# The output projection as side by side 64-row products, in a gated attention unit followed by a token mixer

## The chip, the core and the metric

The kernel runs on one core of a Trainium2 chip. The metric is device time in microseconds (us), from the first to the last instruction of the program on that core. Before the change three runs took 780.02, 781.06 and 780.99 us, median 780.99.

The core has five engines with a queue of instructions each. PE multiplies matrices: it loads weights and streams rows past them, and its sums appear in PSUM. ACT and DVE work element by element, and alone of the engines beside PE read PSUM here. POOL works element by element on SBUF. SP issues most of the transfers. Each engine takes its instructions in the order in which the program gives them, and waits at an instruction until all that it needs is there.

## What is computed

Inputs are u, v (8 x 3200 x 256), z (8 x 3200 x 64) and three small weights. Cut to what matters, for each of the 8 batches:

```
scores = (1 / S) * z @ z.T                 # S = 3200: 3200 x 3200
attn   = max(scores, 0) ** 2
x      = u * (attn @ v)                    # 3200 x 256
wq, wk = x @ w_q, x @ w_k                  # 3200 x 64 each
W_tok  = (1 / 8) * wq @ wk.T
mixed  = W_tok @ x                         # done as wq @ (wk.T @ x)
out    = max(mixed, 0) @ w_out             # 256 x 256 weight: the output projection
```

The change is in the last line: the output projection contracts over the 256 columns of max(mixed, 0).

## The kernel before, in words

Each batch is cut into seven groups of rows: six of 512 and one of 128. For the attention, score tiles are made in pairs (`use_pair`, `scores`, L265): two products of 64 contracted rows, one in the upper half and one in the lower half of the PE array. ACT or DVE takes the pair out of PSUM with a relu (L287, L291), ACT or POOL squares it into one of 16 tiles `at` (L307, L309), and these tiles, or their transposes `tt`, are the weights of the second product with v (L352, `acc`). The second product too runs as two 64-row halves beside each other, r = 0 and r = 1, each into its own bank of PSUM. When a group of rows is summed, ACT and DVE add the two halves (L368, L369), POOL multiplies by u (L388), SP transposes, and PE makes queries and keys (L417) and the heads wk.T @ x (L454), whose sum over the groups is known when the batch ends.

Then, while the attention of the next batch goes on, the batch before is finished group by group. `use_mix` makes mixed.T for a group (L482), ACT takes it out with a relu as `rt` (L503). `use_projs` multiplies `rt` by `wo` (L513): products over all 128 rows of the array, 8 of them for a 512-row group and 2 for the 128-row group, into a buffer `fo` of two banks. ACT or DVE takes `fo` out (L540, L535), and SP stores it. The groups come in twos (`PAIRED`): two 512-row groups are projected in one go, 16 matmuls, each with a buffer of its own.

PSUM has eight banks. Four hold `acc`. The other four are two buffers of two banks, shared by all else: score pairs (`sc`), queries and keys with heads (`qk`), `mx`, `fo`. They come from the pool `pps`, with `bufs=2` and one name, so they are taken in turn, and one is free again when its reader (ACT or DVE) is done.

The order of all instructions is written out beforehand by a planner in the kernel (L575 to L1037). It keeps a clock for each engine, `slots` for the two PSUM buffers, lists of `extras` (keys, heads, mix, proj) with the time from which they may run, and `moves` for SP with due times. At each step the loop at L1001 takes an extra, or a score pair where the supply of `at` tiles is behind (`wanted`), or one step of the second product (`acc_step`, two matmuls). An extra or a pair is taken only when a buffer is free in the planner's count (`room`) and ACT or DVE are free in time for the end of the running sum (`calm_for`). After the loop the last batch is finished in a tail of its own, with `proj` and `mixed` on what is then free.

Of the kernel before, what the change touches and what calls it, by code (L numbers as in the profile page):

```python
# [16 lines left out]
def kernel(  # L17
# [56 lines left out]
    pacc = ctx.enter_context(tc.tile_pool(name="pacc", bufs=1, space=bass.MemoryType.PSUM))  # L74

    def ps_tile(name):
# [47 lines left out]
    def turn_first(c):  # L124
        n0, nn = ZCH[c]
        if c < 3:
            tp = acc_tile((c + 1) // 2 % 2, c % 2, "ztp", FP16)
        else:
            open_slot()
            tp = pps.tile([P, 4 * W], FP16, tag="ps", name="ztp")  # L130
        for i in range(nn):
            nc.tensor.transpose(
                tp[:, ts(i, P)], zd0[:, n0 + i, :, :].rearrange("p a k -> p (a k)"), ident
            )
        clock[PE] += 0.055 * cold() * nn
        ready = clock[PE] + FROM_PE
        on_act = max(clock[ACT], ready) < max(clock[DVE], ready)
        copy = nc.scalar.copy if on_act else nc.vector.tensor_copy
        copy(out=zT[0][:, ds(n0 * P, nn * P)], in_=tp[:, 0 : nn * P])
        z_at[c] = give(ACT if on_act else DVE, ready, 0.16 + 0.07 * nn)  # L140
        if c == 3:
            close_slot(z_at[c])

    def warm(n):
        for _ in range(n):
# [359 lines left out]
    def proj(b, gi, banks):  # L505
        rt = rts.pop((b, gi))
        nj = widths[gi] // P
        for r in halves(gi):
            n = min(2, nj - 2 * r)
            flat = rt[:, r, :, :].rearrange("p d s -> p (d s)")  # L510
            for dc in range(ND):
                for j in range(n):
# [5 lines left out]
                        stop=(dc == ND - 1 and j == n - 1),  # L518
                    )

    def proj_out(b, gi, banks, ways, stores=None, at=0):
        n0 = starts[gi] // P
        if stores is None:
            fo = pg.tile([P, 2, W], FP32, tag="g", name="fo")
        else:
            fo = pg.tile([P, 2, W], FP32, tag="fo", name="fo", bufs=2)
        flat_out = fo[:].rearrange("p a w -> p (a w)")
        for on_dve, queue, n in ways:
            sl = slice(at * D, (at + n) * D)
            if isinstance(banks, list):  # L530
                part = banks[at // 2][:, 0 : n * D]
            else:
                part = banks[:].rearrange("p a w -> p (a w)")[:, sl]
            if on_dve:
                nc.vector.tensor_scalar(  # L535
                    out=flat_out[:, sl], in0=part, scalar1=FINAL_SCALE, scalar2=None,
                    op0=AOP.mult,
                )
            else:
                nc.scalar.mul(out=flat_out[:, sl], in_=part, mul=FINAL_SCALE)  # L540
# [39 lines left out]
        clock[engine] = max(clock[engine], ready) + weight  # L580
        return clock[engine] + HOP

    slots = [0.0, 0.0]
# [4 lines left out]
    mixed_at = []  # L588
    MIXES = 18.0
    MIXES_END = 14.0  # L590
    PAIRED = [0, 1, 2, 3, 4, 5]
    last = B - 1

    moves = []
# [21 lines left out]
    def add_extra(t, kind, fn):  # L616
        extras.append((t, kind, fn))
        extras.sort(key=lambda x: x[0])
# [18 lines left out]
    def close_slot(t):  # L637
        slots.append(t)

    def cold():  # L640
        return 2.0 if clock[PE] < 8.4 else 1.0
# [11 lines left out]
        return a + BIAS < d  # L653

    def use_pair():
        open_slot()
# [12 lines left out]
        g = first_stage(p, sc, ways)  # L669
        close_slot(done)  # L670
        pending.append((done, p, g))

    def squares():
# [34 lines left out]
        double_keys(b, gi)  # L708

    def use_keys(b, gi):  # L710
        open_slot()
        ps = ps_tile("qk")
        prior = None
        if keyed and keys_at.get(keyed[0], 1e9) <= clock[PE]:
# [23 lines left out]
        close_slot(done)  # L738
        if len(keyed) == 2 and gi == LASTG:
            add_extra(done + 14.0, "heads", use_heads)  # L740
        if final:
# [1 line left out]
                add_extra(done, "heads", use_heads)  # L743

    def use_heads():
        open_slot()
# [9 lines left out]
        close_slot(done)  # L756

    def heads_known(b):
        t = clock[PE]
# [2 lines left out]
                add_extra(t + 4.0 + (MIXES if b < last - 1 else MIXES_END) * i, "mix", lambda gi=gi: use_mix(b, gi))  # L762

    def use_mix(b, gi):
        open_slot()
# [5 lines left out]
        close_slot(done)  # L771
# [7 lines left out]
    def use_projs():  # L779
        some = mixed_at[:]  # L780
        mixed_at.clear()
        banks = []
        clock[PE] += 0.22
        for _, b, gi in some:
            open_slot()
            ps = ps_tile("fo")
            proj(b, gi, [ps[:, 0, :], ps[:, 1, :]])
            clock[PE] += 0.86 if gi < LASTG else 0.22
            banks.append((b, gi, ps, clock[PE] + FROM_PE))
        for i, (b, gi, ps, ready) in enumerate(banks):  # L790
            project_out(b, gi, ps, ready)

    def project_out(b, gi, ps, ready):
        stores = []
        on_act = max(clock[ACT], ready) + BIAS <= max(clock[DVE], ready) + 0.2
        proj_out(b, gi, ps, [(not on_act, nc.sync, widths[gi] // P)], stores)
        engine, t = (ACT, 1.0) if on_act else (DVE, 1.23)
        done = give(engine, ready, t if gi < LASTG else 0.3)
        close_slot(done)
        stored.append(1e9)  # L800

        def landed(t, i=len(stored) - 1):
            stored[i] = t

        move(done + SLACK, done + 6.0, 0.55, 1.6, stores[0], landed)

    def push(takes):
        give(POOL, clock[PE], 0.6)
# [139 lines left out]
    def calm_for(kind):  # L948
# [5 lines left out]
        if kind == "keys":  # L954
            return max(clock[ACT], ready + 0.66) + 0.56 <= t
        if kind == "proj":
            n = len(mixed_at)
            return max(clock[ACT], ready + 0.86 * n) + 1.03 <= t
        return max(clock[ACT], ready) + 1.03 <= t

    def p_chunk(p):
# [39 lines left out]
    while groups or work or current["left"]:  # L1001
        flush()
        squares()
        now = clock[PE]
        room = slots[0] <= now
# [12 lines left out]
        if extra and extra[1] == "proj":  # L1018
            room = slots[len(mixed_at) - 1] <= now
        p = produced[0]  # L1020
        able = p < NPAIR and z_here(p) and z_at[p_chunk(p)] <= now and (p < NAT or all_used(p - NAT) and turned_at.get(p - NAT, 0.0) <= now and not out_of.get(p - NAT))
        wanted = able and p * total < (done_acc + lead) * NPAIR
        if room and extra and calm_for(extra[1]) and (not wanted or turn_about or extra[1] == "proj"):
            turn_about = False
            extras.remove(extra)
            extra[2]()
# [5 lines left out]
        elif room and able and calm_for("pair"):  # L1032
            use_pair()
        else:
            marks = slots + [sp_at[0] - 0.4] + [x[0] for x in pending + later + extras + moves]
            marks += list(free_at.values()) + [t for t in row_at.values() if t > now][:50]
            clock[PE] = min([t for t in marks if t > now] + [now + 0.5])  # L1037

    while extras or later or moves:
        x = next((x for x in extras if x[1] == "proj"), None)
        if not x:
            ripe = [
                x
# [13 lines left out]
        else:  # L1059
            extras.remove(x)  # L1060
            x[2]()
    assert not pending and len(keyed) == 1
    def mixed(b, gi, i=None):
        if i is None:
            ps = ps_tile("mx")
# [22 lines left out]
    use_heads()  # L1088
# [57 lines left out]
```

## Time and profile before

| what | value |
|---|---|
| runs | 780.02, 781.06, 780.99 us; median 780.99 |
| profiled execution | 780.02 us; its span from first to last instruction is 780.0 us |
| PE busy | 765.9 us, 98% of the span |
| ACT, DVE, POOL busy | 558.1, 490.5, 619.5 us |
| granted PE clock | 0.998 of full speed over the span |

The profiled execution is the fastest of the three, 0.97 us under the median. In the profile, PE is a row of matmuls and PEld a row of weight loads that run beside them. A matmul of 64 rows is marked 64*128, one over the whole array 128*128. The matmuls are pipelined: a row of one lasts 269 to 273 ns, but the next begins long before it ends, so what a group costs PE is read from the starts of rows that follow each other, not from the sum of their lengths. "Issue" is a wait for which the profile shows no releaser.

### The profile page before, as it was taken

Reading aid. Unit: us, or ns where it says so; the run is one execution under the profiler, and the core shown is the slowest. Engines: PE = TensorE matmul, PEld = TensorE weight load, DVE = VectorE, ACT = ScalarE, POOL = GpSimd, SP = SyncE. Lnnn points to the kernel's source line nnn. Section 1 sums busy time; section 2 is a strip of 40 time slices with the busy share of each in tenths; the row PEclk is TensorE's granted clock in tenths of the full one; section 3 lists DMA queues with packets and bytes.
Section 4 is the critical chain, followed back from the end, with each engine's and each line's share of the span. In section 5 each row is a group of like instructions: output and inputs, shape, how many; then the busy total and the mean of one; then the engine's idle time right before and its main releaser. Section 6 shows DMA issues by size and latency. Waiting matters only on the chain.

```text
span 780.0 us, 28286 instructions
## 1 busy us (share of the span) xinstructions
PE 765.9 (98%) x12410; PEld 674.0 (86%) x12410; DVE 490.5 (63%) x506; ACT 558.1 (72%) x672; POOL 619.5 (79%) x518
## 2 busy tenths in 40 slices
PE   8999999999999999999999999999999999999996
PEld 6889989988888888988889888898888988999894
DVE  6576768767565766655657556575566765656534
ACT  6786785676877776876678777787778578777644
POOL 7798887668986978887779769887888868887850
PEclk9999999999999999999999999999999999999999
DMA  7899999999999999999899999999989999989725
GB/s 181 157 152 175 162 160 170 171 187 180 222 183 190 200 218 204 151 170 217 198 171 193 168 221 168 199 161 171 241 159 208 162 196 211 157 169 168 183 81 198
DMA packets 307116, 141.11 MB, mean 181 GB/s; under 512 B 285744, under 2 KB 288432, under 8 KB 306992
## 3 DMA queue, kind: packets, MB, share of 16 engines
q1 hardware_dynamic: 300224, 123.13, 85.8%
q0 software_dynamic: 6624, 15.98, 14.6%
q8 instruction: 97, 1.59, 0.9%
q14 instruction: 27, 0.22, 0.1%
q10 hardware_dynamic: 144, 0.20, 0.1%
HBM read 59.64 MB, written 26.21 MB: 110 GB/s over the span
## 4 chain that ended last, share of the span: by engine, by line
PE 94%; DVE 2%; DMA 1%; ACT 1%; issue 1%; POOL 0%; DVEq 0%; SPq 0%
PE acc L352 68%; PE sc L265 13%; PE fo L513 6%; PE qk L417 3%; PE qk L454 2%; PE mx L482 1%; DVE g L291 1%; DMA v_sb<-in_v_dram 1%; ACT g L287 1%; DVE both L369 0%; DVE fo L535 0%; DMA z<-in_z_dram 0%; ACT at L307 0%; PE xtx L555 0%; PE hd L454 0%
## 5 line engine op out<-in xcount | busy, mean ns | idle before, releaser
L352 PE MATMUL acc<-v_sb,at 64*128 64x256 f16 x7344 | 506.0, 269 | 2.3 <-issue 1.5
L309 POOL TENSOR_TENSOR at<-g 128x1024 f16<-128x1024 f32 (+2 forms) x240 | 432.5, 1813 | 88.0 <-DVE g L291 46.8
L352 PEld LDWEIGHTS <-at 64*128 64x128 f16 x7344 | 403.9, 94 | 54.5 <-issue 9.7
L291 DVE TENSOR_SCALAR g<-sc 128x1024 f32<-128x1024 f32 (+2 forms) x302 | 349.9, 1175 | 121.8 <-PE sc L265 109.8
L307 ACT ACTIVATE at<-g 128x1024 f16<-128x1024 f32 (+2 forms) x242 | 241.6, 1015 | 25.0 <-DVE g L291 22.5
L287 ACT ACTIVATE g<-sc 128x1024 f32<-128x1024 f32 (+2 forms) x177 | 174.8, 990 | 56.2 <-PE sc L265 50.9
L265 PE MATMUL sc<-zT 64*128 64x512 f16 x924 | 185.3, 375 | 2.4 <-DVE g L291 1.2
L388 POOL TENSOR_TENSOR x_sb<-both,u_sb 128x512 f16<-128x512 f32 (+1 forms) x112 | 134.3, 1205 | 48.9 <-DVE both L369 48.4
L352 PE MATMUL acc<-v_sb,tt 64*128 64x256 f16 x2272 | 168.0, 269 | 0.0
L352 PEld LDWEIGHTS <-tt 64*128 64x128 f16 x2272 | 127.0, 94 | 10.3 <-issue 0.6
L369 DVE TENSOR_TENSOR both<-acc,both 128x512 f32<-128x512 f32 (+1 forms) x104 | 69.5, 670 | 70.9 <-ACT both L368 62.0
L368 ACT COPY both<-acc 128x512 f32<-128x512 f32 (+1 forms) x104 | 58.9, 566 | 66.5 <-PE acc L352 63.1
L265 PEld LDWEIGHTS <-zT 64*128 64x128 f16 x924 | 62.2, 94 | 9.8 <-issue 5.2
L535 DVE TENSOR_SCALAR fo<-fo 128x1024 f32<-128x1024 f32 (+2 forms) x31 | 32.7, 1067 | 41.4 <-PE fo L513 41.3
L503 ACT ACTIVATE rt<-mx 128x1024 f16<-128x1024 f32 (+1 forms) x49 | 45.5, 931 | 12.2 <-PE mx L482 12.0
L430 ACT CAST qk<-qk 128x512 f16<-128x512 f32 (+1 forms) x54 | 29.4, 544 | 29.2 <-PE qk L454 25.4
L513 PE MATMUL fo<-wo,rt 128*128 128x256 f16 x400 | 49.4, 273 | 0.1
L469 DVE TENSOR_TENSOR ha<-qk,ha 128x512 f32<-128x512 f32 x37 | 25.6, 691 | 36.1 <-ACT qk L430 35.8
L513 PEld LDWEIGHTS <-rt 128*128 128x128 f16 x400 | 36.4, 98 | 10.8 <-issue 6.5
L540 ACT ACTIVATE fo<-fo 128x1024 f32<-128x1024 f32 (+2 forms) x27 | 24.6, 914 | 19.8 <-PE fo L513 19.8
L417 PE MATMUL qk<-xT_sb,wqk 64*128 64x256 f16 (+1 forms) x404 | 32.2, 265 | 0.0
L454 PE MATMUL qk<-x_sb,kx 64*128 64x256 f16 x360 | 29.1, 269 | 0.0
(44 smaller groups left out, 237.0 us busy)
## 6 DMA issues: line engine op xcount, KB each, us to landing
u_sb<-in_u_dram SPq DMA_DIRECT2D x48, 512.0 KB, 5.0
out_dram<-fo SPq DMA_DIRECT2D x46, 512.0 KB, 4.4
v_sb<-in_v_dram POOLq DMA_DIRECT2D x35, 320.0 KB, 6.2
zn<-in_z_dram POOLq DMA_DIRECT2D x7, 400.0 KB, 6.3
tt<-at SPq DMA_TRANSPOSE x143, 4.5
u_sb<-in_u_dram SPq DMA_DIRECT2D x8, 128.0 KB, 3.6
out_dram<-fo SPq DMA_DIRECT2D x8, 128.0 KB, 3.5
out_dram<-fo SPq DMA_DIRECT2D x4, 256.0 KB, 4.2
```

The lines of the kernel that those rows point to most:

```text
L265: nc.tensor.matmul(out=sc[:, h, 0:gw], lhsT=z_cols(b, h, ti * P, P), rhs=z_cols(b, h, gs, gw), start=True, stop=True,)
L287: nc.scalar.activation(out=g[:, hs, 0:w], in_=sc[:, hs, 0:w], func=RELU, scale=GSCALE)
L291: nc.vector.tensor_scalar(out=g[:, hs, 0:w], in0=sc[:, hs, 0:w], scalar1=0.0, scalar2=GSCALE, op0=AOP.max, op1=AOP.mult,)
L307: nc.scalar.square(out=out, in_=g[:, hs, 0:w])
L309: nc.gpsimd.tensor_mul(out=out, in0=g[:, hs, 0:w], in1=g[:, hs, 0:w])
L352: nc.tensor.matmul(out=accs[half, r][:, ds((j % 2) * D, D)], lhsT=weights(b, gi, ti, j)[top(r), :], rhs=vs[b][top(r), ti, :], start=(first ...
L368: nc.scalar.copy(out=both[:, 0 : n * D], in_=accs[half, 0][:, 0 : n * D])
L369: nc.vector.tensor_add(out=both[:, 0 : n * D], in0=accs[half, 1][:, 0 : n * D], in1=both[:, 0 : n * D])
L388: nc.gpsimd.tensor_mul(out=xs[b, gi][:, 0:n, :, r, :].rearrange("p n c d -> p (n c) d"), in0=both[:, 0 : n * D].rearrange("p (m d) -> p m ...
L417: nc.tensor.matmul(out=ps[:, r, 0 : n * P], lhsT=wqk[top(r), c, :, :].rearrange("p t h -> p (t h)"), rhs=xTs[b, gi][top(r), 0:n, c, :], st ...
L503: nc.scalar.activation(out=out, in_=ps[:, 0:nr, 0 : ND * n * P], func=RELU)
L513: nc.tensor.matmul(out=banks[r][:, ds(j * D, D)], lhsT=flat[:, ds((dc * n + j) * P, P)], rhs=wo[:, dc, :], start=(dc == 0 and j == 0), sto ...
```

## The change

Three things change together. The output projection of the first seven batches is cut into 64-row products. The projection of a 512-row group becomes two phases of 8 matmuls (`proj_phase`). In the first, rows 0 to 63 of the array work on bank 0 and rows 64 to 127 on bank 1. In the second, the halves change banks. Each bank so gets the sum over both halves. Between the phases stands a copy of two numbers out of the two banks (`mark`), on ACT or DVE, which the second phase waits for. The buffer stays taken from the first phase until the result is out. The 128-row group (`use_small_proj`) lets each half write its own bank and ACT and DVE add the two.

The groups are projected one by one instead of in twos: `PAIRED` and `mixed_at` go, the first phase is an extra `proj`, the second an extra `proj2`. `proj2` may run without a free buffer, since it has one, but in the planner it waits until the store before the last has landed (`stored[-2] + 2.0`). A mix may run while fewer than two groups are mixed and not yet projected out.

The two PSUM buffers get names, `ps0` and `ps1`, each a pool of one. `open_slot` takes the one that is free first by the planner's count.

```diff
-    pps = ctx.enter_context(tc.tile_pool(name="pps", bufs=2, space=bass.MemoryType.PSUM))
+    pps = ctx.enter_context(tc.tile_pool(name="pps", bufs=1, space=bass.MemoryType.PSUM))
...
     def ps_tile(name):
-        return pps.tile([P, 2, W], FP32, tag="ps", name=name)
+        if ending:
+            slot[0] = 1 - slot[0]
+        return pps.tile([P, 2, W], FP32, tag=f"ps{slot[0]}", name=name)
...
+    def proj_phase(b, gi, ps, crossed):
+        rt = rts.pop((b, gi)) if crossed else rts[b, gi]
+        for i, (dc, j) in enumerate((dc, j) for dc in range(ND) for j in range(2)):
+            for r in range(2):
+                bank = 1 - r if crossed else r
+                flat = rt[:, bank, :, :].rearrange("p d s -> p (d s)")
+                nc.tensor.matmul(
+                    out=ps[:, bank, ds(j * D, D)],
+                    lhsT=flat[top(r), ds((dc * 2 + j) * P, P)],
+                    rhs=wo[top(r), dc, :],
+                    start=(not crossed and i == 0),
+                    stop=(i == 3),
+                    skip_group_check=crossed,
+                )
+
+    def proj_parted(b, gi, ps):
+        flat = rts.pop((b, gi))[:, 0, :, :].rearrange("p d s -> p (d s)")
+        for dc in range(ND):
+            for r in range(2):
+                nc.tensor.matmul(
+                    out=ps[:, r, 0:D],
+                    lhsT=flat[top(r), ts(dc, P)],
+                    rhs=wo[top(r), dc, :],
+                    start=(dc == 0),
+                    stop=(dc == ND - 1),
+                )
...
     def open_slot():
-        clock[PE] = max(clock[PE], slots.pop(0))
+        slot[0] = k = min(slots, key=lambda k: slots[k])
+        clock[PE] = max(clock[PE], slots[k])
+        slots[k] = 1e9
+        return k
...
-        mixed_at.append((done, b, gi))
-        if gi in PAIRED:
-            if len(mixed_at) == 2:
-                add_extra(done + 0.5, "proj", use_projs)
-        else:
-            add_extra(done + 0.5, "proj", use_projs)
...
+        unprojected.append(gi)
+        use = use_proj if gi < LASTG else use_small_proj
+        add_extra(done + 0.5, "proj", lambda: use(b, gi))
+
+    def use_proj(b, gi):
+        k = open_slot()
+        ps = ps_tile("fo")
+        proj_phase(b, gi, ps, False)
+        clock[PE] += 0.44
+        mark = psml.tile([1, 2], FP32, tag="mark", name="mark")
+        ready = clock[PE] + FROM_PE
+        on_act = clock[ACT] < min(clock[DVE], shut())
+        copy = nc.scalar.copy if on_act else nc.vector.tensor_copy
+        copy(out=mark[:], in_=ps[0:1, :, D])
+        done = give(ACT if on_act else DVE, ready, 0.2)
+        add_extra(done + 0.2, "proj2", lambda: use_proj2(b, gi, k, ps))
+
+    def use_proj2(b, gi, k, ps):
+        proj_phase(b, gi, ps, True)
+        clock[PE] += 0.44
...
+        proj_out(b, gi, ps, [(not on_act, nc.sync, widths[gi] // P)], stores)
+        done = give(ACT, ready, 1.0) if on_act else give(DVE, ready, 1.23)
+        projected_out(k, done, stores[0])
+
+    def use_small_proj(b, gi):
+        k = open_slot()
+        ps = ps_tile("fo")
+        proj_parted(b, gi, ps)
...
+        nc.scalar.mul(out=fo[:, 1, 0:D], in_=ps[:, 1, 0:D], mul=FINAL_SCALE)
+        nc.vector.scalar_tensor_tensor(
+            out=fo[:, 0, 0:D], in0=ps[:, 0, 0:D], scalar=FINAL_SCALE,
+            in1=fo[:, 1, 0:D], op0=AOP.mult, op1=AOP.add,
+        )
...
-                and (x[1] != "proj" or all(t + 2.0 <= now for t in stored[-2:][: len(mixed_at)]))
+                and (x[1] != "proj2" or len(stored) < 2 or stored[-2] + 2.0 <= now)
                 and (x[1] != "heads" or keys_at.get(keyed[0], 1e9) <= now)
-                and (x[1] != "mix" or not any(y[1] == "proj" for y in extras))
+                and (x[1] != "mix" or len(unprojected) < 2)
...
-        if room and extra and calm_for(extra[1]) and (not wanted or turn_about or extra[1] == "proj"):
+        if (room or extra and extra[1] == "proj2") and extra and calm_for(extra[1]) and (not wanted or turn_about or extra[1] == "proj2"):
```

More of the change, by code (lines that the diff above doesn't have):

```diff
@@ L128, in turn_first @@
         else:
-            open_slot()
-            tp = pps.tile([P, 4 * W], FP16, tag="ps", name="ztp")
+            k = open_slot()
+            tp = pps.tile([P, 4 * W], FP16, tag=f"ps{k}", name="ztp")
         for i in range(nn):
@@ L793, in project_out @@
[L793 to L799, printed above, removed]
+        close_slot(k, done)
+        unprojected.append(gi)
+        use = use_proj if gi < LASTG else use_small_proj
+        add_extra(done + 0.5, "proj", lambda: use(b, gi))
@@ new lines, in use_proj2 @@
+    def use_proj2(b, gi, k, ps):
+        proj_phase(b, gi, ps, True)
+        clock[PE] += 0.44
+        ready = clock[PE] + FROM_PE
+        on_act = max(clock[ACT], ready) + BIAS <= max(clock[DVE], ready) + 0.2
+        stores = []
+        proj_out(b, gi, ps, [(not on_act, nc.sync, widths[gi] // P)], stores)
+        done = give(ACT, ready, 1.0) if on_act else give(DVE, ready, 1.23)
+        projected_out(k, done, stores[0])
+    def use_small_proj(b, gi):
+        k = open_slot()
+        ps = ps_tile("fo")
+        proj_parted(b, gi, ps)
+        clock[PE] += 0.22
+        fo = pg.tile([P, 2, W], FP32, tag="fo", name="fo", bufs=2)
+        nc.scalar.mul(out=fo[:, 1, 0:D], in_=ps[:, 1, 0:D], mul=FINAL_SCALE)
[3 more added lines that the diff above has]
+        )
+        done = give(DVE, give(ACT, clock[PE] + FROM_PE, 0.35), 0.4)
+        n0 = starts[gi] // P
+        projected_out(
+            k, done, lambda: nc.sync.dma_start(out=rows(out, b)[:, n0, :], in_=fo[:, 0, 0:D])
+        )
@@ L800, in project_out, with projected_out @@
+    def projected_out(k, done, store):
+        close_slot(k, done)
+        unprojected.pop(0)
         stored.append(1e9)
@@ L803, in landed @@
             stored[i] = t
-        move(done + SLACK, done + 6.0, 0.55, 1.6, stores[0], landed)
+        move(done + SLACK, done + 6.0, 0.55, 1.6, store, landed)
     def push(takes):
@@ L956, in calm_for @@
         if kind == "proj":
-            n = len(mixed_at)
-            return max(clock[ACT], ready + 0.86 * n) + 1.03 <= t
+            return True
+        if kind == "proj2":
+            ready += 0.22
+            return max(clock[ACT], ready) + 1.03 <= t or max(clock[DVE], ready) + 1.23 <= t + 0.69
         return max(clock[ACT], ready) + 1.03 <= t
@@ L1004 @@
         now = clock[PE]
-        room = slots[0] <= now
+        room = min(slots.values()) <= now
         extra = next(
@@ L1017 @@
         )
-        if extra and extra[1] == "proj":
-            room = slots[len(mixed_at) - 1] <= now
         p = produced[0]
@@ L1034 @@
         else:
-            marks = slots + [sp_at[0] - 0.4] + [x[0] for x in pending + later + extras + moves]
+            marks = list(slots.values()) + [sp_at[0] - 0.4] + [x[0] for x in pending + later + extras + moves]
             marks += list(free_at.values()) + [t for t in row_at.values() if t > now][:50]
@@ L1041 @@
     while extras or later or moves:
-        x = next((x for x in extras if x[1] == "proj"), None)
+        x = next((x for x in extras if x[1] in ("proj", "proj2")), None)
         if not x:
@@ L1061 @@
             x[2]()
-    assert not pending and len(keyed) == 1
+    assert not pending and len(keyed) <= 1
+    ending.append(True)
     def mixed(b, gi, i=None):
@@ L1087 @@
     nc.scalar.copy(out=g32[1][:], in_=psg[1][:, 0:D])
-    use_heads()
+    if keyed:
+        use_heads()
     hsum = pg.tile([P, D], FP32, tag="g", name="hm")
```

39 lines of the change are left out of this document (13 added, 26 removed).

## The prediction

> **What bounds the kernel now.** I read the page first, its busy shares and its chain, then the busy times by stage, then who waited for whom, and last the rows in order of time around one projection.
>
> ```profile
> span 780.0 us, 28286 instructions
> PE 765.9 (98%) x12410; PEld 674.0 (86%) x12410; DVE 490.5 (63%) x506; ACT 558.1 (72%) x672; POOL 619.5 (79%) x518
> PE 94%; DVE 2%; DMA 1%; ACT 1%; issue 1%; POOL 0%; DVEq 0%; SPq 0%
> ```
>
> PE is busy for 98% and is 94% of the chain that ended last. Next, the busy time by stage (window, its length, busy us and count of each engine, granted clock, DMA share, GB/s):
>
> ```profile
> 160.00:460.00 300.00, 299.47 (x4913) 258.75 (x4908) 187.61 (x191) 222.39 (x261) 241.57 (x199) 1.00 1.08 192
> 460.00:757.00 297.00, 296.93 (x4852) 263.05 (x4852) 181.22 (x186) 214.92 (x256) 246.51 (x201) 1.00 0.96 175
> ```
>
> From 160 to 757 us, where the projections lie, PE stands idle for 0.6 us in all, at a granted clock of 1.00. So whatever PE no longer has to do there is won, and whatever makes it wait there is lost one for one. Two groups of waits of the weight loads show time inside this busy PE:
>
> ```profile
> PEld L352 <- issue: 10.5, 35, 1.8
> PEld L513 <- issue: 6.5, 31, 0.2
> ```
>
> Both sides of the projection have a gap without a releaser, 0.21 us before L513 (6.5 / 31) and about as much behind it, as the rows around the first projection show:
>
> ```profile
> 157.35 0.61 PE L352 MATMUL acc<-v_sb,at 64*128 64x256 f16 x8
> 157.90 1.92 PE L513 MATMUL fo<-wo,rt 128*128 128x256 f16 x16
> 158.98 1.02 ACT L540 ACTIVATE fo<-fo 128x1024 f32<-128x1024 f32 x1 [0.27 <-PE fo L513]
> 159.75 0.72 PE L352 MATMUL acc<-v_sb,at 64*128 64x256 f16 x10
> 159.86 1.22 DVE L535 TENSOR_SCALAR fo<-fo 128x1024 f32<-128x1024 f32 x1 [1.38 <-PE fo L513]
> 160.31 0.38 PE L265 MATMUL sc<-zT 64*128 64x512 f16 x2
> 160.52 0.27 PE L352 MATMUL acc<-v_sb,at 64*128 64x256 f16 x2
> 160.79 1.02 ACT L287 ACTIVATE g<-sc 128x1024 f32<-128x1024 f32 x1 [0.78 <-PE sc L265]
> ```
>
> The gap appears where the form goes from 64*128 to 128*128 and back, and not between lines that are both 64*128.
>
> **The change part by part.** First the pace of a side by side pair, and a place where PE did wait for a product buffer:
>
> ```profile
> 408.07 0.61 PE L265 MATMUL sc<-zT 64*128 64x512 f16 x4
> 408.50 1.23 DVE L291 TENSOR_SCALAR g<-sc 128x1024 f32<-128x1024 f32 x1 [0.48 <-PE sc L265]
> 409.78 0.69 PE L265 MATMUL sc<-zT 64*128 64x512 f16 x4 [0.23 <-DVE g L291]
> 410.29 1.92 PE L352 MATMUL acc<-v_sb,at 64*128 64x256 f16 x32
> 412.03 0.40 PE L265 MATMUL sc<-zT 64*128 64x512 f16 x2
> ```
>
> *Pace.* 32 matmuls of L352 take 412.03 - 410.29 = 1.74 us, 0.109 us for two beside each other. The 16 whole-array matmuls of the block at 157.90 take 1.85 us to the next row, gap included. So two halves side by side cost what one whole product costs, and the 350 matmuls that become 700 (42 groups x 16, 7 x 4) cost PE the same 38 us. Their weight loads double too, but two load beside each other as those of L352 do: no cost.
>
> *The change of form.* The 8 matmuls at 157.35 are four pairs and fill PE to 157.79. The next row behind the projection starts at 159.75. The block thus takes 1.96 us; 16 pairs would take 16 x 0.109 = 1.74. That is 0.22 us for a block, whatever its size. Of the 32 blocks in the written order 28 become 64-row (the last four, in the tail, stay): 28 x 0.22 = **-6.2 us**. Ends: 28 x 0.21 for the gap in front alone, 5.9, and 28 x 0.42 with both gaps in full, 11.8. I take 6.2, read from a whole block.
>
> The Trainium skill, in its page "TensorEngine Tiling (Array Packing)", section "Instruction Overhead", gives each matmul some 60 cycles of overhead. By that the 350 added matmuls would cost, as an estimate at the 2.4 GHz that "Trainium Kernel Development and Optimization" (section "NeuronCore Architecture") states, 350 x 25 ns = 8.8 us, more than the change of form saves. The trace does not agree for this shape: 0.109 us for two halves of 256 columns, the same as for one whole product.
>
> *The copies.* 42 copies of two numbers, 25 on ACT and 17 on DVE in the written order. The trace has none so small; the nearest are these:
>
> ```profile
> L430 ACT CAST qk<-qk 128x128 f16<-128x128 f32 x7 | 1.9, 266 | 3.8 <-PE qk L454 3.7
> L291 DVE TENSOR_SCALAR g<-sc 128x128 f32<-128x128 f32 x6 | 1.7, 282 | 1.2 <-PE sc L265 1.2
> L540 ACT ACTIVATE fo<-fo 128x1024 f32<-128x1024 f32 x22 | 22.4, 1024 | 17.5 <-PE fo L513 17.5
> L535 DVE TENSOR_SCALAR fo<-fo 128x1024 f32<-128x1024 f32 x24 | 29.2, 1224 | 39.1 <-PE fo L513 39.1
> L503 ACT ACTIVATE rt<-mx 128x1024 f16<-128x1024 f32 x42 | 42.8, 1022 | 11.6 <-PE mx L482 11.4
> L309 POOL TENSOR_TENSOR at<-g 128x1024 f16<-128x1024 f32 x220 | 414.5, 1894 | 86.1 <-DVE g L291 45.3 <-ACT g L287 32.0 <-issue 4.0
> out_dram<-fo SPq DMA_DIRECT2D x46, 512.0 KB, 4.4
> ```
>
> At most 0.28 us each, so 12 us over two engines that stand idle for over 200 us each; at least nothing. What is queued behind such a copy is a copy out of `acc` or a score pair, late by 0.28 us at most. The second phase waits for the copy: 0.27 from PE to the reader, 0.28, and 0.05 back (409.73 to 409.78 above), 0.6 us. In the written order other PE work stands between the phases, 0.87 us or more, in all but one of the 42 groups. Direct cost 0.6 us or less in all; I take zero, the cover being those steps of L352.
>
> *The 128-row groups.* One more ACT and one DVE instruction of a 256-column tile, seven times, off the chain: zero. *Stores.* As many as before, one by one in place of two at a time; SP gets no more work: zero, but see the rivals.
>
> *The buffer that is held.* This is the large term. Before, a projection holds a buffer from its first matmul to the end of the copy out: 157.90 to 160.00 us for the first group (158.98 + 1.02), about 158.8 to 161.08 for the second, 2.1 and 2.3 us. After, from the first phase to the end of the copy out behind the second. In the written order the PE work from the start of a group's first phase to the end of its second is between 1.3 and 11.9 us, 5.5 in the mean, and 0.27 + 1.02 + 0.05 = 1.34 us follow for an ACT copy: 6.9 us. For 42 groups that is some 195 us more of buffer time, and there are two buffers in all. While one is held, every score pair, mix and key product must go through the other, which is back no sooner than this:
>
> - a score pair with DVE: 408.07 to 409.78, 1.71 us; with ACT: 160.31, copied from 160.79 to 161.81, plus 0.05, 1.55 us.
> - a mix: 0.22 + 0.27 + 1.02 + 0.05 = 1.56 us (L503).
>
> Score matmuls by window before (62 are 31 pairs):
>
> ```profile
> 157.00:205.00 48.00, 12.16 (x62) 3.80 (x62) 1.00 1.05 200
> ```
>
> Before, 31 pairs are made in the 48 us of a batch's projections. In the changed order, 20 pairs stand in the 47.5 us of PE work from the first phase of the same batch to its last. The rest comes later, in rows of `sc` with little or no second product between them: `sc4`, `sc10` and `sc12`, where before it never has more than four score matmuls in a row. Here one such stretch, in the written order, with the buffer behind the @ (F2 is a second phase, numbers count steps of L352):
>
> ```
> F2@1  13  sc@1  2  mx@1  F2@0  sc@1  mx@0  sc@1  qk@0  sc@1  11
> ```
>
> Each opening against the one before on its buffer: mx@1 1.71 us after sc@1, with 0.43 us of PE work between, 1.28 short; sc@1 1.56 - 0.66 = 0.90 short; mx@0 1.34 behind F2's end, of which 1.12 have gone, 0.22; sc@1 1.71 - 0.69 = 1.02; qk@0 1.56 - 1.46 = 0.10; sc@1 1.71 - 1.19 = 0.52. Sum 4.0 us in which PE has nothing to do. Counted so for every opening, and with the tiles that L352 lacks behind such a stretch (1.71 and 1.9 us on POOL for a pair), the seven batches are short by 8.2, 7.9, 8.7, 8.2, 6.9, 3.9 and 10.2 us: **+54.0 us**. The same count on the order before gives 6.2 us where the trace shows 0.6 us idle, so it is some 6 too high; on the other hand it lets every copy start at once, though ACT and DVE have other work in their queues, and lets each `fo` tile be free, though a store needs 4.4 us to land. I leave the two against each other. Bounds: half the count (PE reaches each place with more tiles in hand), 27; one and a half times, 81.
>
> *Buffers by name.* Taking the one that is free first, not the next in turn, can only spare such waits, and they were 0.6 us: zero. *The tail.* Its `hd` product now falls in the loop: under 1 us, left out.
>
> **Sum.** 780.0 - 6.2 + 54.0 = 827.8 us. The profiled execution is 1.0 us under the median of its runs; with that, 828.8, said as 828.
>
> **The rivals.** *Only the change of form counts (faster).* If steps of L352 and the 16 tiles in store cover every held buffer, 781 - 6.2 = 774.8 us. For it: PE has the tiles in store, and ACT and DVE have idle time. Against: 11 of 31 pairs are missing in a window, and rows like `sc@1 mx@1` can't be covered, as nothing stands between. It decides if fewer than 6.2 of the 54 us come true. Chance 0.04.
>
> *Half covered.* The stretches cost once, not also as lacking tiles behind them: 27 - 6.2, 802 us. Chance 0.14.
>
> *Stores and queues add to it (slower still).* The copy out of a second phase must find one of two `fo` tiles free. Where SP, behind its transposes, sends a store late, the copy waits on ACT or DVE with all that is queued behind it, and the buffer is held for longer: 81 - 6.2, 856 us. Against: the planner puts a second phase behind the landing of the store before last. Chance 0.10.
>
> *The halves do not run beside each other in this product*, because they change banks: 350 more matmuls of 0.109 us, 38 us, on top of the forecast, 866 us; without the held buffers 813. Against: L352 does the same with two banks at 0.109 us a pair. Chance 0.02.
>
> **How the numbers follow.** The forecast, 828 us, has 0.70. The range, 799 to 856 us, reaches from half the count to one and a half times and leaves out the faster case and the ends. Runs of this kernel differ by 0.13%, so 0.2% is about what can be told from no change. Faster 0.04; within 0.2% 0.02, where held buffers and change of form cancel; slower 0.94.
>
> **What would show it.** Right: no gap of 0.2 us before the projection's weight loads; pairs of it at 0.109 us; PE waits for DVE and ACT at L265, L482 and L417 under their new numbers, some 50 us in all, in the seven stretches behind the projections; a granted clock of 1.00 throughout. The copies near 0.25 us, the second phase seldom waiting for them. Wrong: PE idle in those stretches under 6 us, or a wait of PE for the copies, or SP's stores as the releaser of ACT and DVE.

## The result, and the profile after

The changed kernel takes 844.57 us (median of 840.94, 848.2, 848.87 and 839.1) against 780.5 us: 1.081 times as long, 95% interval 1.075 to 1.086. The forecast was 828, range 799 to 856, slower with 0.94. The profiled execution has a span of 839.1 us, 59.1 us more than the one before.

The page of the changed kernel: span, busy shares, the chain that ended last.

```profile
span 839.1 us, 29092 instructions
PE 786.6 (94%) x12760; PEld 712.9 (85%) x12760; DVE 505.3 (60%) x536; ACT 548.7 (65%) x681; POOL 634.7 (76%) x528
PE 78%; DVE 6%; ACT 5%; DMA 4%; POOL 2%; issue 2%; SPq 1%; DVEq 0%; POOLq 0%; ACTq 0%
```

PE was 94% of the chain and is 78%. The rest now goes through DVE, ACT and transfers, the ways by which a product buffer comes back. Busy time by stage (columns as before), over the batches in which the projections lie:

```profile
150.00:480.00 330.00, 313.92 (x5100) 281.95 (x5098) 189.96 (x202) 218.08 (x264) 246.72 (x203) 0.97 1.02 177
480.00:818.00 338.00, 314.70 (x5186) 287.46 (x5182) 199.53 (x212) 215.77 (x267) 261.71 (x210) 0.98 0.86 160
```

PE's row is idle for 39.4 us here, where it was 0.6. The granted clock is 0.97 and 0.98, where it was 1.00. Who waited (us in total, times, longest), and the new copies and phases:

```profile
PEld L269 <- issue: 36.5, 57, 1.5
PEld L486 <- issue: 9.3, 13, 3.0
PEld L421 <- issue: 7.1, 11, 1.5
PE sc L269 <- DVE g L295: 13.9, 22, 1.2
L531 PE MATMUL fo<-wo,rt 64*128 64x256 f16 x672 | 50.2, 269 | 1.5 <-DVE g L295 1.0 <-ACT rt L507 0.5
L818 ACT COPY mark<-fo 1x2 f32<-1x2 f32 x25 | 3.7, 149 | 45.3 <-PE fo L531 43.9
```

L269, L486 and L421 are the score pairs, the mixes and the key products: the openings of product buffers. PE never waits for L818, the copy between the phases. Now the stretch that the forecast worked through, in order of time:

```profile
181.13 1.02 ACT L571 ACTIVATE fo<-fo 128x1024 f32<-128x1024 f32 x1 [4.55 <-DMA out_dram<-fo]
182.20 0.39 PE L269 MATMUL sc<-zT 64*128 64x512 f16 x2 [0.69 <-ACT fo L571]
182.63 1.23 DVE L295 TENSOR_SCALAR g<-sc 128x1024 f32<-128x1024 f32 x1 [6.99 <-PE sc L269]
183.91 0.21 PE L486 MATMUL mx<-qk,hs 64*128 64x128 f16 x1 [1.10 <-DVE g L295]
184.66 1.02 ACT L571 ACTIVATE fo<-fo 128x1024 f32<-128x1024 f32 x1
184.71 0.37 PE L269 MATMUL sc<-zT 64*128 64x512 f16 x2
185.73 0.61 PE L486 MATMUL mx<-qk,hs 64*128 64x256 f16 x4 [0.65 <-ACT fo L571]
186.15 0.62 PE L269 MATMUL sc<-zT 64*128 64x512 f16 x2
187.51 1.03 PE L421 MATMUL qk<-xT_sb,wqk 64*128 64x256 f16 x8 [0.74 <-ACT rt L507]
```

From the score pair to the mix on the same buffer 1.71 us pass, as forecast. From 182.20 to 187.51, 5.31 us, PE has some 1.6 us of work at full clock; the forecast had it 3.5 us short up to that place, it is 3.7. The links are not all as forecast: the score pair behind the mix comes after 0.80 us in place of 1.56 (the mix is that of the 128-row group, whose copy is short), the key products 1.78 us behind their mix in place of 1.56, and about 0.4 of the 3.7 us is work at half the clock, on which more below. DVE had waited 6.99 us for a score pair: both buffers were held, one by a group between its phases, one by the copy out at 181.13, which itself waited for a store to land. In the 48 us around the first batch's projections, 31 pairs were made before; now 38 score matmuls stand there, 19 pairs (busy us of L269, PE and PEld):

```profile
150.00:198.00 48.00, 7.77 (x38) 2.56 (x38) 0.93 1.00 176
```

What the forecast did not have is the clock. Six stretches run at half of it:

```profile
185.30:192.10 6.80, 5.62 (x48) 3.76 (x49) 2.71 (x4) 3.47 (x5) 4.36 (x6) 0.50 0.50 178
301.40:308.20 6.80, 5.84 (x42) 3.44 (x43) 3.94 (x4) 4.47 (x5) 6.53 (x8) 0.50 0.96 172
...
sum 30.60, PE 26.48 PEld 17.76 DVE 14.99 ACT 17.70 POOL 24.83; mean PE 4.41 PEld 2.96 DVE 2.50 ACT 2.95 POOL 4.14
```

PE is busy in 26.5 of these 30.6 us; at the full clock that work would take 13 to 14 us less. The 3.41 us ahead of each of the six:

```profile
181.89:185.30 3.41, 1.69 (x18) 0.92 (x18) 1.33 (x2) 1.29 (x3) 1.30 (x1) 1.00 1.28 153
...
809.99:813.40 3.41, 1.20 (x14) 0.57 (x13) 1.37 (x3) 1.02 (x1) 2.85 (x2) 0.99 0.37 154
sum 20.46, PE 8.74 PEld 4.13 DVE 12.07 ACT 13.38 POOL 12.85; mean PE 1.46 PEld 0.69 DVE 2.01 ACT 2.23 POOL 2.14
```

PE was busy for 1.20 to 1.69 us in each, under half, in short pieces.

The sum for the profiled execution: 59.1 = -6.2 for the change of form, +13.7 at half clock, +51.6 of waits. The last two can be counted from the starts of the matmuls, at 0.109 us for a pair of 256 columns and 0.216 us for a score pair. Both kernels have 749.6 us of such work. Beside it stand 30.4 us in the span before and 75.8 us in the span after; the work inside the six stretches takes 13.7 us longer than at full clock.

### The profile page after: what moved, and what is told of

Same layout as the page of the kernel before. It is cut to its first block, busy times and chain, and to the rows that moved or that the text cites. A ratio compares the mean times of both kernels' runs of the same rounds, so it can differ in the third digit from the quotient of the medians.

```text
span 839.1 us, 29092 instructions
## 1 busy us (share of the span) xinstructions
PE 786.6 (94%) x12760; PEld 712.9 (85%) x12760; DVE 505.3 (60%) x536; ACT 548.7 (65%) x681; POOL 634.7 (76%) x528
## 4 chain that ended last, share of the span: by engine, by line
PE 78%; DVE 6%; ACT 5%; DMA 4%; POOL 2%; issue 2%; SPq 1%; DVEq 0%; POOLq 0%; ACTq 0%
PE acc L356 57%; PE sc L269 11%; DVE g L295 4%; PE fo L531 4%; PE qk L421 3%; DMA out_dram<-fo 3%; PE qk L458 2%; POOL at L313 2%; ACT g L291 2%; PE mx L486 1%; ACT fo L571 1%; DMA v_sb<-in_v_dram 1%; ACT at L311 1%; DVE both L373 1%; ACT both L372 1%
## 5 line engine op out<-in xcount | busy, mean ns | idle before, releaser
L356 PE MATMUL acc<-v_sb,at 64*128 64x256 f16 x7344 | 520.3, 272 | 5.4 <-POOL at L313 2.7
L313 POOL TENSOR_TENSOR at<-g 128x1024 f16<-128x1024 f32 (+2 forms) x250 | 446.1, 1798 | 97.4 <-DVE g L295 67.5
L295 DVE TENSOR_SCALAR g<-sc 128x1024 f32<-128x1024 f32 (+1 forms) x323 | 373.7, 1175 | 164.0 <-PE sc L269 148.0
L356 PEld LDWEIGHTS <-at 64*128 64x128 f16 x7344 | 428.3, 95 | 41.4 <-issue 8.2
L269 PE MATMUL sc<-zT 64*128 64x512 f16 x924 | 192.3, 383 | 24.3 <-DVE g L295 13.9
L291 ACT ACTIVATE g<-sc 128x1024 f32<-128x1024 f32 (+2 forms) x156 | 154.6, 992 | 46.6 <-PE sc L269 40.1
L356 PE MATMUL acc<-v_sb,tt 64*128 64x256 f16 x2272 | 170.3, 269 | 0.0
L356 PEld LDWEIGHTS <-tt 64*128 64x128 f16 x2272 | 134.0, 94 | 4.3
L269 PEld LDWEIGHTS <-zT 64*128 64x128 f16 x924 | 67.4, 95 | 40.2 <-issue 36.5
L531 PE MATMUL fo<-wo,rt 64*128 64x256 f16 x672 | 50.2, 269 | 1.5 <-DVE g L295 1.0
L571 ACT ACTIVATE fo<-fo 128x1024 f32<-128x1024 f32 (+1 forms) x35 | 35.5, 1014 | 16.3 <-PE fo L531 8.7
L531 PEld LDWEIGHTS <-rt 64*128 64x128 f16 x672 | 37.6, 94 | 3.5 <-issue 2.8
L421 PE MATMUL qk<-xT_sb,wqk 64*128 64x256 f16 (+1 forms) x404 | 33.5, 271 | 4.0 <-ACT g L291 2.2
L451 POOL COPY kx<-kx 128x128 f16<-128x128 f16 (+1 forms) x99 | 25.8, 289 | 11.1 <-DMA kx<-qk 11.1
L818 ACT COPY mark<-fo 1x2 f32<-1x2 f32 x25 | 3.7, 149 | 45.3 <-PE fo L531 43.9
```

Source lines behind the costliest of these rows:

```text
L269: nc.tensor.matmul(out=sc[:, h, 0:gw], lhsT=z_cols(b, h, ti * P, P), rhs=z_cols(b, h, gs, gw), start=True, stop=True,)
L291: nc.scalar.activation(out=g[:, hs, 0:w], in_=sc[:, hs, 0:w], func=RELU, scale=GSCALE)
L295: nc.vector.tensor_scalar(out=g[:, hs, 0:w], in0=sc[:, hs, 0:w], scalar1=0.0, scalar2=GSCALE, op0=AOP.max, op1=AOP.mult,)
L313: nc.gpsimd.tensor_mul(out=out, in0=g[:, hs, 0:w], in1=g[:, hs, 0:w])
L356: nc.tensor.matmul(out=accs[half, r][:, ds((j % 2) * D, D)], lhsT=weights(b, gi, ti, j)[top(r), :], rhs=vs[b][top(r), ti, :], start=(first ...
L421: nc.tensor.matmul(out=ps[:, r, 0 : n * P], lhsT=wqk[top(r), c, :, :].rearrange("p t h -> p (t h)"), rhs=xTs[b, gi][top(r), 0:n, c, :], st ...
```

## The experiments

The theory: a product buffer held from the first phase to the end of the second starves the score pairs. Rivals: the groups taken one by one, or the named buffers; the 64-row form itself; the copies; the landing of stores. All times below are medians, beside 780.3 to 780.8 us for the kernel before in the same sessions; ratios are to it.

**One by one, but as one whole-array product.** No second phase, no copy, nothing held:

```diff
+    def use_proj(b, gi):
+        k = open_slot()
+        ps = ps_tile("fo")
+        clock[PE] += 0.22
+        proj(b, gi, [ps[:, 0, :], ps[:, 1, :]])
...
+        projected_out(k, done, stores[0])
```

> Groups one by one and named buffers as in the changed kernel, but the 512-row group as one whole-array product (8 matmuls over 128 rows) with no second phase and no copy. If the buffer held between the two phases starves the score pairs: 780 to 786 us, PE idle under 5 us between 150 and 750 us, granted clock 1.00. If taking groups one by one or the named buffers is what costs: 820 us or more.

783.36 us, ratio 1.003 (1.000 to 1.006), granted clock 0.998. PE's row is idle for 0.25 us from 150 to 750 us. Neither the order one by one nor the named buffers is what costs. For the 3 us that are left the trace shows more changes of form: 50 gaps ahead of the projection's weight loads, 10.5 us, where there were 31, 6.5 us.

**Second phase straight behind the copy, and the same with steps of the second product in the gap:**

```diff
-        add_extra(done + 0.2, "proj2", lambda: use_proj2(b, gi, k, ps))
+        while clock[PE] < done + 0.2 and acc_step():     # in the second kernel only
+            steps_between[0] += 1
+        clock[PE] = max(clock[PE], done + 0.2)
+        use_proj2(b, gi, k, ps)
```

Two more rules of the planner, not shown, differ from the changed kernel. In both, as in the kernel just above, the wait for the landed store moves ahead of the (first) product, and a projection goes ahead of a wanted score pair, if ACT or DVE will be free for its copy out.

> The changed kernel with the second phase put straight behind the copy, no other PE work between. If the held buffer is the cause: the starved stretches go, the mean hold falls from about 7 to 3 us, and what is left is PE waiting some 0.5 us for each of 42 copies (21 us) less the 6 us of the change of form: 790 to 800 us, waits of PE for L818 showing that. If the 64-row form itself (halves not side by side, or the doubled weight loads) costs: 835 us or more.

> As e2_adjacent, but the wait for the copy is filled with steps of the second product where there are any (about eight). Held-buffer theory: better than e2_adjacent by part of its 21 us, 776 to 795 us. If the copies or the crossing of banks cost on PE in themselves: no better than e2_adjacent.

794.19 us (1.018, 1.014 to 1.022) and 796.22 us (1.020, 1.017 to 1.023). The first is as forecast. Two phases with nothing between, in order of time:

```profile
149.46 0.61 PE L531 MATMUL fo<-wo,rt 64*128 64x256 f16 x8
150.11 0.15 DVE L819 COPY mark<-fo 1x2 f32<-1x2 f32 x1 [0.70 <-PE fo L531]
150.31 0.61 PE L531 MATMUL fo<-wo,rt 64*128 64x256 f16 x8 [0.24 <-DVE mark L819]
```

0.85 us from phase to phase, of which four pairs take 0.44: a copy costs PE 0.41 us when nothing covers it, 17 us over 42 groups, less 6 for the change of form. The mean hold is 2.7 us. The second kernel is a miss, by 1.2 us, and no better than the first, which is what was said for copies or crossed banks that cost PE in themselves. Two kernels below have the same copies and crossing and take 778.30 and 776.75 us, so it is not these. Nor is it the length of the hold, 3.1 us here and 3.2 us in the one at 778.30. Against that kernel the weight loads wait 6.7 us more for L531 (the copies), 8.4 us more for L269 (the score pairs) and 3.9 us more for L356 (the second product). Which rule of the order causes this, no run shows.

**The same order, held buffers and all, but each phase a whole-array product for one bank:**

```diff
-                bank = 1 - r if crossed else r
-                flat = rt[:, bank, :, :].rearrange("p d s -> p (d s)")
+        bank = int(crossed)
+        flat = rt[:, bank, :, :].rearrange("p d s -> p (d s)")
...
-                    lhsT=flat[top(r), ds((dc * 2 + j) * P, P)],
-                    rhs=wo[top(r), dc, :],
+                lhsT=flat[:, ds((dc * 2 + j) * P, P)],
+                rhs=wo[:, dc, :],
```

> The changed kernel's order kept as it is, held buffers included, but each phase is a whole-array product of 128 rows for one bank (4 matmuls), so there are no side by side halves. Held-buffer theory: the same starved stretches as in the changed kernel, plus up to 84 phases x 0.22 us of change of form, some of it hidden in waits: 845 to 865 us. If the 64-row form is what costs: 800 us or less.

851.3 us, 1.089 (1.084 to 1.094). Without any 64-row projection of a 512-row group the loss stays: it is not the form. By the medians the side by side form is worth 6.7 us in this order, but the two intervals touch.

**Shorter holds.** In the changed kernel a second phase waits for the landed store while it holds its buffer, two groups may be held at once, and a second phase takes its turn among the extras:

```diff
-                for x in extras
+                for x in sorted(extras, key=lambda x: (x[1] != "proj2", x[0]))
                 if x[0] <= now
...
-                and (x[1] != "proj2" or len(stored) < 2 or stored[-2] + 2.0 <= now)
+                and (x[1] != "proj" or len(held) < 1 and (len(stored) < 2 or stored[-2] + 2.0 <= now))
```

(`held` has the groups between their phases.) One kernel has both lines, one only the first, one only the second.

> The changed kernel, groups one by one, copies, named buffers and other work between the phases kept; but the wait for the landed store stands ahead of the first phase in place of the second, one group is held at a time, and a second phase goes ahead of all other extras. Held-buffer theory: mean hold 3 to 4 us in place of 7.3, no starved stretches, clock 1.00: 775 to 786 us. If putting work between the phases, the named buffers or the one by one order starve the pairs even so: 800 us or more.

> The changed kernel with only the last of these three: a second phase goes ahead of other extras, still behind the landed store. If the time follows the length of the hold: between the two, 790 to 815 us, mean hold 4.5 to 6 us.

> e8_prompt without the rule that a second phase goes ahead of other extras; the wait for the landed store stays ahead of the first phase and one group is held at a time. If the wait for the store while the buffer is held was most of the loss: 780 to 795 us, mean hold under 4.5 us. If the order among the extras was most of it: over 800 us.

| kernel | mean hold of a buffer, us | time, us | ratio (95%) |
|---|---|---|---|
| changed kernel | 7.2 | 844.57 | 1.081 (1.075 to 1.086) |
| second phase first among extras | 5.1 | 809.76 | 1.037 (1.033 to 1.040) |
| store waited for ahead of the first phase, one held | 4.1 | 785.62 | 1.007 (1.005 to 1.010) |
| both | 3.2 | 778.30 | 0.997 (0.996 to 0.999) |

The hold is taken from each trace, from the first matmul of the first phase to the end of the copy out, the mean of 42 groups. All four kernels have the same 64-row products, copies and buffers, and among them the time follows the hold. What falls with the mean is also the time in which two groups hold both buffers at once, 71, 34, 0 and 1 us down the table; these runs don't tell the two apart. Nor does a short hold alone make a fast kernel, as the one at 796.22 us shows. Where both lines are in, PE's row is idle for 2.8 us over the stage in place of 39.4, at full clock:

```profile
150.00:460.00 310.00, 307.82 (x5244) 289.70 (x5242) 205.89 (x215) 220.00 (x274) 258.64 (x210) 1.00 1.11 189
460.00:755.00 295.00, 294.34 (x5041) 277.58 (x5038) 190.58 (x204) 206.56 (x255) 246.36 (x199) 1.00 0.95 179
```

**The change of form by itself.** The order of the kernel with both lines, with whole-array halves as above:

> The order and the buffers of e8_prompt to the instruction, but each phase is a whole-array product of 128 rows for one bank, as in e4_held_whole. Where nothing hides it, the change of form at 84 phases and 7 small groups costs 91 x 0.2 us: 794 to 798 us. If much of the change of form is hidden even in a full PE, or the side by side form has a cost of its own: under 788 us.

795.44 us against 778.30: 17.1 us. The 7 small groups are 64-row products in both kernels, so it is 84 phases that change the form there and back, not 91: 0.20 us each. The gaps stand where the form changes (L530 is the projection, L356 the second product):

```profile
PEld L356 <- issue: 19.8, 77, 0.8
PEld L530 <- issue: 19.1, 83, 0.3
```

**The kernel before with only the form changed,** groups in twos:

```diff
+        for i, (_, b, gi) in enumerate(some):
+            open_slot()
+            ps = ps_tile("fo")
+            proj_phase(b, gi, ps, False)
...
+            copy(out=mark[:], in_=ps[0:1, :, D])
...
+        for b, gi, ps in held:
+            proj_phase(b, gi, ps, True)
```

> The kernel before with its groups in twos and its buffers in turn, only the form changed: first phase of one group, first phase of the other, second phase of the one, second phase of the other, with the two copies, nothing else between. The other group's first phase (0.44 us) covers the copy. Buffers are held about as long as before. If the change of form is worth 0.22 us a block: 774 to 777 us. If the second phases wait for copies that stand in ACT's or DVE's queue, 0.4 us or more in each of 21 blocks: 782 to 790 us.

783.95 us, 1.004 (1.003 to 1.006): a miss; the time is in the range of the second guess, but not by its cause. The copies are covered: the block of 32 matmuls of the first two groups takes 1.75 us, as it should. But behind it:

```profile
156.62 1.93 PE L527 MATMUL fo<-wo,rt 64*128 64x256 f16 x32
158.15 1.02 ACT L567 ACTIVATE fo<-fo 128x1024 f32<-128x1024 f32 x1 [0.60 <-PE fo L527]
158.37 0.72 PE L352 MATMUL acc<-v_sb,at 64*128 64x256 f16 x10
159.22 0.39 PE L265 MATMUL sc<-zT 64*128 64x512 f16 x2
```

The ten matmuls, five pairs, need 0.55 us, the next score pair comes 0.85 us behind their start: it waits 0.3 us for the first group's buffer, whose copy out ends at 159.17. The first group is now finished only behind the second one's first phase, and PE is there 0.2 us sooner. That wait of about 0.3 us stands behind 19 of the 21 blocks, some 6 us, about as much as the change of form saves. It explains why nothing is won; the 3 us by which this kernel is slower than the one before (783.95 against 780.75) it leaves open.

**PE kept busy.** The order of the changed kernel with some 260 pairs of products by zeros, put where its planner lets PE wait:

```diff
+                nc.tensor.matmul(
+                    out=accs[0, r][:, 0:D], lhsT=zero[top(r), :], rhs=vs[b][top(r), 0, :],
+                    start=False, stop=False, skip_group_check=True,
+                )
```

> The changed kernel's order with some 260 pairs of products by a weight of zeros put into the running sums, at the places where its planner lets PE wait (29 us of extra PE work that changes no value). If the stretches at half clock are a cost of their own, set off by PE's waiting: granted clock back to 1.00 and 825 to 838 us, less than the changed kernel's 844.6 although PE does more. If the half clock lies under waits and costs nothing, or the filling takes the place of no wait: 845 to 870 us.

840.78 us, 1.075 (1.071 to 1.079), a little less than the changed kernel, intervals overlapping, and between the two guesses: a miss for both. The profiled execution is the fastest of the four, 833.8 us. There the granted clock is back at 0.996 (one stretch of 3.4 us at half in place of six, 30.6 us). Counted as above, PE does 28.9 us more, 24.2 us of it in place of waits, and 11.8 us less are lost at half clock: the span is 7.1 us shorter, 832.0 us. The other three give back less of the clock, and the time goes with it: 843.85 us at 0.985, 841.22 at 0.988, 840.34 at 0.991, 833.8 at 0.996. So the half clock has a price of its own; four runs are few to say how large.

**Stores from another tile,** so that no copy out waits for a landing:

```diff
-                in_=flat_out[:, sl].rearrange("p (n d) -> p n d", d=D),
+                in_=blank[:].rearrange("p (n d) -> p n d", d=D).broadcast_to([P, n, D]),
```

> The changed kernel's order, held buffers and all, but the stores of the first seven batches send a tile of zeros, of the same size and at the same place in SP's queue, so no copy out of a projection waits for a store to land and SP waits for no copy (the output of these batches is left out). If the landing of stores adds to the loss beside the held buffers: 825 to 838 us, the waits of ACT for the out transfer gone. If the buffers held by the written order are all of it: 840 to 849 us.

838.13 us, 1.072 (1.069 to 1.076), a hair above the first guess's range. In the changed kernel ACT waits twice for the landing of an `out` transfer, 6.9 us, before copies out of 512-row groups, and twice before those of the 128-row groups:

```profile
L571 ACT ACTIVATE fo<-fo 128x1024 f32<-128x1024 f32 x34 | 34.9, 1026 | 15.7 <-PE fo L531 8.7 <-DMA out_dram<-fo 6.9
L838 ACT ACTIVATE fo<-fo 128x256 f32<-128x256 f32 x7 | 2.7, 383 | 6.3 <-DMA out_dram<-fo 4.4 <-PE fo L544 1.8
```

In this kernel ACT has no wait for an `out` transfer. The time is 6 us lower at the median, at the edge of what the intervals tell apart. The landing of stores adds little; 58 of 64 us stay without it.

**A second order.** The kernel with both lines, and the planner's cost of a copy set to 0.15 us:

> e8_prompt with the planner's cost of a copy set to the 0.15 us that the traces show, in place of 0.2. No theory tells a time apart here; a second order with the same rules, to see whether the gain of e8_prompt hangs on one lucky order: 775 to 781 us if it does not, over 784 us if it does.

776.75 us, 0.995 (0.993 to 0.996): the gain does not hang on one order. This is the fastest of all kernels here.

## Why the prediction was right, and where it was short

*The change of form, -6.2 us, 0.22 us a block.* Right: 0.20 us each in a full PE. In the changed kernel no wait of 0.2 us stands ahead of each block of L531 any more (2.8 us in 7 waits in all).

*350 more matmuls for nothing.* Right: four pairs in 0.44 us (149.71 to 150.15 in the changed kernel's trace):

```profile
149.71 0.61 PE L531 MATMUL fo<-wo,rt 64*128 64x256 f16 x8
150.15 0.61 PE L356 MATMUL acc<-v_sb,tt 64*128 64x256 f16 x8
```

The rival of the halves that don't run beside each other falls with it.

The rule that the prediction took from the Trainium skill, page "TensorEngine Tiling (Array Packing)", section "Instruction Overhead", adds nothing to the time of these matmuls: eight of them take the 0.44 us of four whole products at 0.109 us.

*The copies.* 0.149 us on ACT, inside the bounds 0 to 0.28 though not near the 0.25 that was to be looked for, and covered, as said. Uncovered a copy costs 0.41 us, not the 0.6 of the forecast.

*The held buffer.* Right, and it decides: 7.2 us mean hold measured, 6.9 forecast; +51.6 us of waits, 54.0 forecast; some 50 us were looked for at the openings of buffers, and the weight loads of L269, L486 and L421 wait 36.5 + 9.3 + 7.1 = 52.9 us. The runs with shorter holds show that it is the held buffer. By batch the waits, counted as above, are 7.6, 6.1, 8.5, 9.0, 6.2, 6.9 and 9.4 us, where 8.2, 7.9, 8.7, 8.2, 6.9, 3.9 and 10.2 were forecast: the sum is nearer than its parts.

*A granted clock of 1.00 throughout.* This is the step that failed: 30.6 us at half clock, 13.7 us of PE time. On the profiled execution, with a span of 839.1 us against the 827.8 of the sum, that is more than the whole miss, as the waits are 2.4 us fewer than forecast. The other 5 us up to the median of 844.57 lie between this execution's span and the median run. The forecast had read the clock off a profile in which PE never waited, and carried it into a stage for which it predicted that PE would. The Trainium skill has a case like it, in its page "TensorE: Matmul & The Clock Gate", section "A second HAM failure mode: psum-queue depth-cycling": in a kernel that cycles through PSUM banks in each iteration, PE idles briefly between groups of matmuls, often enough that its clock goes back and forth between half and full. The trace agrees that short idle spells are enough: each of the six stretches follows 3.41 us with PE busy for under half.

*Stores and queues.* Given 0.10 as a rival, and set against an overcount in the main sum. They exist, at 6 us or less. That the two were about of one size was not worked out; it is luck that the sum of 54.0 came so near.

*The 1.0 us for the median.* It takes the span of 780.0 us for the run of 780.02 us. In every run here that has both, the time is 1.7 to 1.9 us longer than the span, so that execution isn't shown to be the fastest of the three. The spans, 780.0 and 839.1 us, can be compared. And 828.8 is nearer to 829 than to the 828 that was said.

*Only the change of form counts,* the faster rival, came true for other kernels: in the two fastest, with mean holds of 3.2 and 3.1 us, PE keeps its work and the gain is 2 to 4 us. Why not the whole 6, the runs don't show.

## What to carry to other kernels

When a step is cut in two with a buffer kept between, count the buffer's time and not only the engine's: with two buffers in all, a long hold was paid for by everyone else who needed one. Put any wait that can be long (here the landing of a store) ahead of taking the buffer, and finish what is begun before anything else. And a forecast of new waits on PE has to ask for the clock as well: what PE does after such a spell may run at half speed, as it did here for 30.6 us.

## What was not expected

PE lost half its clock without a long idle spell. In the 3.41 us ahead of each half-clock stretch PE was busy for 35% to 50%, and no gap between the starts of two matmuls there is over 1.7 us. The one long gap, 3.1 us (the 3.0 us in the row of L486 above, from 692.4 to 695.5 us), was followed by no half clock.

Where the stretches begin fits this. They start at 185.3, 301.4, 407.2, 513.0, 789.5 and 813.4 us, whole multiples of 3.413 us apart (34, 31, 31, 81 and 7), and last one or two of these steps. Cut on this grid, the whole trace of the changed kernel, up to the end of its last matmuls, has six windows in which PE's row is busy for half or less, and they are the six that half clock follows; the next have 52%. The long gap falls across two windows, neither under 52%:

```profile
690.48:693.89 3.41, 2.20 (x39) 1.90 (x34) 1.30 (x2) 0.41 (x1) 1.89 (x1) 1.00 0.95 271
693.89:697.30 3.41, 1.77 (x32) 1.66 (x33) 1.56 (x2) 1.41 (x2) 0.61 (x1) 1.00 1.01 309
```

In the kernel with the second phase straight behind the copy, a gap of 3.9 us fills one window, and the next runs at half clock:

```profile
179.67:183.08 3.41, 0.18 (x4) 0.00 (x0) 0.32 (x1) 0.65 (x1) 1.89 (x1) 1.00 0.62 136
183.08:186.50 3.42, 3.00 (x26) 2.12 (x27) 1.23 (x1) 1.87 (x3) 0.40 (x1) 0.50 1.15 263
```

Busy for half is not an exact limit: in the kernel at 851.3 us, with a whole-array product for each phase, a window with 47% was followed by no half clock, one with 48% was.

Where the clock came into play the runs also spread: 839.1 to 848.87 us, 1.2%, where the four runs of the kernel before beside them spread over 0.2%. The granted clock of these four lies between 0.979 and 0.981, so the clock alone doesn't tell them apart.
